# A fourth group of the u table by seven part products, its sums made on VectorE; checks moved behind other work; the last tile in its own banks

## Chip, cores and metric

One core of one Trainium2 chip runs the whole program. The metric is the device time of one execution in microseconds (us). The kernel before takes 1130.21 us, the median of three runs (1128.66 to 1132.23). TensorE is called PE here, VectorE DVE, ScalarE ACT, GpSimd POOL; SP (SyncE) issues nearly all DMAs.

## The reference

Two branches are added to the input x (2048 tokens of 512 values), both fed by its layer norm xn:

```
a, b = xn @ dft_hid_re.T, xn @ dft_hid_im.T
y    = dft_seq_re @ a - dft_seq_im @ b                 # Fourier mixing
q    = xn @ w_q                                        # 32 heads, two halves of 128
s1, s2 = q1 @ k1.T, q2 @ k2.T                          # 64 scores each, best 2 of each
top 2 of the 4 sums per head -> 64 expert numbers a token and softmax gates g
act  = gelu(xn . u[e]);  out = sum g * act * v[e]      # 4096 experts, u and v 4096 x 512
result = x + y + out
```

## The kernel before, in words

The tokens are cut into 16 blocks of 128. After a DFT part (to about 102 us) comes the **score stage** (102 to 429 us): 128 steps (eight score columns j by 16 blocks i), each 12 fp16 matmuls of 512 columns on PE, one eviction on ACT (line 952), eight MAX8 and two searches on DVE (lines 956, 960). Scores wait in 4 PSUM banks and 4 SBUF buffers, so DVE can fall some blocks behind PE. Beside it, u and v are read and split into a high and a low fp16 part: ACT writes the high parts and a scaled copy (780, 781), POOL subtracts (782).

Instead of gathering experts, the kernel then forms z = xn @ u.T for **all** 4096 experts, gates it, and multiplies with all of v. The u table has 16 groups of 256 experts. Blocks 0 and 1 are done alone (`u_part`, line 1095); then seven cycles follow, each a **pair** of blocks in z (7 x 41 us) and then two v stretches (together 45 us), `v(b-1)` and `v(b)`, and at the end `v(15)`.

Within a pair, four groups and two blocks make a 2x2 matrix product, done in Winograd's way: seven part products of 24 matmuls with 128 columns (`slot`, line 1173) instead of eight. `SEQ` writes their order by hand: `1a 5a 2a 6a c 3a ...`, where the digit is one of the seven products (`OPS`), the letter one of three such quads, and `c` a plain group (0 to 3) by `u_part`, 24 matmuls with 256 columns for both blocks at once. Between products ACT copies the running sum X out of PSUM (lines 1213, 1218, 1220, 1226: after 1, 5, 6 and 7), DVE adds (1215, 1223, 1227), ACT applies gelu (1203); product 7 must wait until the copy after 6 has read X, and 4 for the copy after 7. Products 3, 6 and 7 need sums of four u parts, which are made before, in the score stage (`sum_u`, lines 809 to 812, and `split4`, 794 and 795), kept in HBM as `s_d` and loaded by SP into a ring of three 512 KB buffers (`ring_load`, line 1156).

The gates come as `g_mm` (line 1270): DVE builds two halves, each a mask L (1260) and a weighted mask R (1265, then 1268), and PE multiplies them, 32 matmuls of 32 columns. There are three L and R buffers and two PSUM buffers for g. `w_part` then multiplies act by g (1278, DVE), rounds (1285, ACT) and takes the rest (1286, DVE). The call g(b,1) is made by `put(ph, 12, ...)` inside the pair.

Between all this stand **checks** that inputs are what the fast path assumes. A unit of U (`compare`, lines 1350 to 1405; the last four `compare_w`) reads a piece of a DFT matrix (0.5 MB), takes differences on DVE and one sum of absolute values on ACT (1404). A unit of F[0] (`fit`, 1451) reads 0.5 MB of w_q, or later of v, and takes one such sum on ACT (1456). F[1] does so for resident parts of u and v (1467). The places are listed as `put(phase, position, unit)`. Loads of both kinds and the tiles of `w_part` share four buffers (tag "w").

Every engine works its list strictly in order; a scheduler makes the lists when the program is built.

## Time and profile before

| | |
|---|---|
| median of three runs | 1130.21 us (1128.66 to 1132.23) |
| profiled execution | 1130.3 us, of which the span on the engines is 1128.0 |
| granted TensorE clock | 0.999 |
| busy share of the span | PE 98%, DVE 86%, ACT 59%, POOL 29% |
| data moved | 206.80 MB |

Times in the tables are microseconds from the start of the span. A timeline row gives start, duration, engine, line, operation, output and inputs, the number of instructions put together in the row, and in brackets the idle time before it with what ended it. PE's durations overlap each other, so a stretch of PE is measured from one start to the next.

### The profile page before, as it was taken

To read this page: it belongs to the slowest core of one execution; us is meant where nothing else is said; L and a number is where in the kernel's file an instruction comes from. 1 tells how busy PE (TensorE), PEld (TensorE's weight loads), DVE (VectorE), ACT (ScalarE), POOL (GpSimd) and SP (SyncE) were. 2 spreads that over 40 slices of the span, in tenths; PEclk is the share of its full clock that TensorE was granted. 3 is DMA by queue.
4 is the path that set the end of the run, shared out by engine and by line. 5 is a ranking of instruction groups with operands and counts; after the bars stand their busy time and mean duration, and the time that the engine had idled before them with its cause. 6 is when DMAs were issued, how large, how long until landed. Compare 5 with 4: busy or idle time off the path is not lost.

```text
span 1128.0 us, 28019 instructions
## 1 busy us (share of the span) xinstructions
PE 1109.6 (98%) x11024; PEld 720.0 (64%) x11024; DVE 965.1 (86%) x2883; ACT 667.7 (59%) x1118; POOL 328.6 (29%) x364
## 2 busy tenths in 40 slices
PE   9999999999999999999999999999999999999997
PEld 6455554544545459678479479579469569559643
DVE  7899989989889899885997996997997897887892
ACT  6557698798898465365546545535545635545442
POOL 1415998888889750000000010010010010000000
PEclk9999999999999999999999999999999999999999
DMA  9984456346353215663754854753745755655353
GB/s 285 286 209 164 162 182 202 116 156 200 97 182 111 97 52 187 214 218 118 265 205 153 255 209 141 259 203 146 272 165 189 236 192 197 225 197 188 105 186 107
DMA packets 123932, 206.80 MB, mean 183 GB/s; under 512 B 34564, under 2 KB 65419, under 8 KB 123790
## 3 DMA queue, kind: packets, MB, share of 16 engines
q1 hardware_dynamic: 123488, 204.84, 54.7%
q8 instruction: 88, 1.44, 0.5%
q14 instruction: 54, 0.44, 0.1%
q10 hardware_dynamic: 302, 0.08, 0.0%
HBM read 171.52 MB, written 27.59 MB: 177 GB/s over the span
## 4 chain that ended last, share of the span: by engine, by line
PE 46%; DVE 12%; DMA 3%; ACT 3%; POOL 2%; issue 1%; SPq 0%; ACTq 0%; DVEq 0%; POOLq 0%
PE v L1328 18%; PE z L1173 16%; PE z L1095 9%; PE g L1270 3%; DVE L L1260 2%; DVE w L1278 2%; DMA cx<-in_cb_dram 2%; DVE vals L956 1%; DVE act L1286 1%; DVE idx L960 1%; DMA fit<-in_wq_dram 1%; DVE w L1286 1%; DVE cx L1378 1%; DVE R L1265 1%; DMA v<-v_d 1%
## 5 line engine op out<-in xcount | busy, mean ns | idle before, releaser
L252 PE MATMUL s<-m,xq 128*128 128x512 f16 x1344 | 297.4, 379 | 1.0 <-ACT ss L952 0.5
L1328 PE MATMUL v<-v,act 128*128 128x512 f16 x1044 | 230.8, 379 | 0.3 <-DMA v<-v_d 0.3
L252 PEld LDWEIGHTS <-xq 128*128 128x128 f16 x1344 | 129.8, 98 | 152.2 <-issue 2.5
L1341 POOL TENSOR_TENSOR y<-y,xr 128x512 f32<-128x512 f32 x15 | 28.7, 1915 | 637.9 <-DMA y<-y_d 455.8
L1260 DVE TENSOR_TENSOR L<-io_lam,cmp 128x2048 f16<-128x2048 f16 x128 | 156.1, 1220 | 26.0 <-PE g L1270 25.9
L1328 PEld LDWEIGHTS <-act 128*128 128x128 f16 x1044 | 100.1, 98 | 116.5 <-issue 0.6
L956 DVE MAX8 vals<-ss 128x8 f32<-128x64 f32 x896 | 133.5, 216 | 3.9 <-ACT ss L952 3.9
L1095 PE MATMUL z<-xb,u 128*128 128x128 f16 (+1 forms) x1440 | 121.8, 244 | 0.1
L1173 PEld LDWEIGHTS <-u 128*128 128x128 f16 x2016 | 114.7, 98 | 3.1 <-issue 2.6
L1095 PEld LDWEIGHTS <-u 128*128 128x128 f16 x1440 | 107.6, 98 | 7.5 <-issue 0.2
L1328 PE MATMUL v<-v,w 128*128 128x512 f16 x480 | 106.3, 379 | 0.3 <-DMA v<-v_d 0.3
L952 ACT ACTIVATE ss<-s,wsc 128x512 f32<-128x512 f32 x120 | 81.4, 683 | 38.6 <-PE s L252 33.4
L1404 ACT ACTIVATE cx<-cx 128x896 f32<-128x896 f32 x64 | 60.5, 946 | 67.7 <-DVE cx L1384 38.1
L960 DVE FIND_INDEX8 idx<-vals,ss 128x8 uint16<-128x256 f32 x224 | 93.8, 419 | 0.0
L1173 PEld LDWEIGHTS <-s 128*128 128x128 f16 x1440 | 82.5, 98 | 0.2
L1328 PEld LDWEIGHTS <-w 128*128 128x128 f16 x480 | 46.0, 98 | 53.8 <-issue 0.6
L1285 ACT ACTIVATE act<-w 128x1024 f16<-128x1024 f32 x36 | 48.3, 1358 | 53.8 <-DVE w L1278 49.4
L1270 PEld LDWEIGHTS <-L 128*128 128x128 f16 x2048 | 60.5, 96 | 15.6 <-DVE R L1268 4.2
L1270 PE MATMUL g<-R,L 128*128 128x32 f16 x2048 | 62.0, 176 | 4.3 <-DVE R L1268 4.2
L1278 DVE SCALAR_TENSOR_TENSOR w<-act,scl,g 128x1024 f32<-128x1024 f32 x44 | 55.8, 1277 | 10.3 <-ACT act L1203 10.3
L1173 PE MATMUL z<-xb,u 128*128 128x128 f16 x1008 | 63.1, 219 | 0.4 <-ACT act L1102 0.3
L1173 PE MATMUL z<-x,u 128*128 128x128 f16 x1008 | 61.3, 219 | 1.6 <-ACT w L1226 0.8
(366 smaller groups left out, 1860.8 us busy)
## 6 DMA issues: line engine op xcount, KB each, us to landing
v<-v_d SPq DMA_DIRECT2D x67, 512.0 KB, 4.6
cx<-in_cb_dram SPq DMA_DIRECT2D x64, 448.0 KB, 6.1
s<-s_d SPq DMA_DIRECT2D x42, 512.0 KB, 3.1
w<-in_wq_dram SPq DMA_DIRECT2D x28, 512.0 KB, 6.3
fit<-in_wq_dram SPq DMA_DIRECT2D x28, 512.0 KB, 4.7
uv<-in_vn_dram SPq DMA_DIRECT2D x16, 512.0 KB, 3.8
uv<-in_ut_dram SPq DMA_DIRECT2D x16, 512.0 KB, 4.0
s_d<-v SPq DMA_DIRECT2D x24, 256.0 KB, 4.1
```

Of the source, the lines that this page charges most:

```text
L252: nc.tensor.matmul(ps, xt[i][:, l, kd, :], m[:, r, kd, :], start=(n == 0), stop=(n == 3 * KD - 1))
L952: nc.scalar.activation(s, ps, AF.Copy, scale=inv)
L956: nc.vector.max(vals[:, i, w, :, h], s[:, g, :])
L960: nc.vector.max_index(idx[:, i, w].rearrange("p k h -> p (k h)"), vals[:, i, w, 0:2].rearrange("p k h -> p (k h)"), s[:, w * HC:g + 1, :]. ...
L1095: nc.tensor.matmul(ps if n == 1 else ps.rearrange("p (b n) -> p b n", b=2), ug[:, l, c % 2, kd, :], xb2[:, k0, r, kd, :] if n == 1 else xb ...
L1173: nc.tensor.matmul(bank[:, t * P:(t + 1) * P], lt, rt, start=(t == k == 0 and op in "125"), stop=(t == 3 and k == 5), skip_group_check=op ...
L1260: nc.vector.tensor_tensor(L.rearrange("p t (l two) -> p t l two", two=2), io_lam.rearrange("p (l two) -> p l two", two=2).unsqueeze(1).to_ ...
L1270: nc.tensor.matmul(p[:, hf, t * NC:(t + 1) * NC], L[:, t, :], R[:, t, :], start=True, stop=True)
L1278: nc.vector.scalar_tensor_tensor(w, act[:, :, ts], fw, p.rearrange("p h (n c) -> p c (h n)", c=NC), op0=ALU.mult, op1=ALU.mult)
L1285: nc.scalar.activation(w16[..., 0], w, AF.Copy)
L1328: nc.tensor.matmul(pv, w16[:, c, :, l], v_sb[g][:, r, cc, :], start=(n + cc == 0 and k == 0), stop=(n == end and cc == 1 and k == 2))
L1404: later.append(lambda: nc.scalar.activation(tf[:, P:], tf[:, P:], AF.Abs, accum_out=chk[:, n:n + 1]))
```

## The change

Four parts. **First**, groups 0 to 3 become a fourth quad; the plain groups are gone from the pairs, `SEQ` has 28 products, and g(b,1) stands as `g` between the last 7 and the last 4. The sums of these groups are made in the score stage, by DVE in place of POOL, in the scratch of tiles of v; ACT and POOL split them like the others. **Second**, the w_q checks leave the pairs and half of those of v(0) leave too; they go to position 3 of each odd v stretch and to the start of v(2) and v(4). **Third**, the difference checks are placed anew; the last three come behind the last weights of block 15. **Fourth**, the last two 256-column halves of block 15 each get a PSUM bank of their own, after a first addition into y.

```diff
 XS = 512.0
 V1 = 5
 V2 = 9
-QUADS = (8, 10, 12, 14), (9, 11, 13, 15), (4, 5, 6, 7)
+QUADS = (0, 1, 2, 3), (8, 10, 12, 14), (9, 11, 13, 15), (4, 5, 6, 7)
 PAIRS = tuple(range(2, NT, 2))
 
 
...
             nc.gpsimd.tensor_tensor(dl, raw, dh, op=ALU.subtract)
             if which == 0 and not safe and any(g in q for q in QUADS):
                 SRAW[g] = raw
-                sum_u(g, 0)
+                if g > 3:
+                    sum_u(g, 0)
 
         def scratch(g):
             return v_sb[g].rearrange("p l c d -> p (l c d)").bitcast(F32)
...
         def sum_u(g, part, at=None):
 
             qd, t = next((n, q.index(g)) for n, q in enumerate(QUADS) if g in q)
-            par = [f for w, f in fills if w == 0 and any(f in q for q in QUADS)].index(g) % 2
-            s4 = scratch(8 - par)
+            par = [f for w, f in fills if w == 0 and f > 3].index(g) % 2 if g > 3 else g % 2
+            s4 = scratch(8 - par if g > 3 else g)
+            hi = v_sb[4 if g in (2, 3) else 6].rearrange("p l c d -> p (l c d)")
+            eng = nc.gpsimd if g > 3 else nc.vector
             if part == 0:
                 raw = SRAW.pop(g)
                 a = [raw[:, c, k * 256:k * 256 + 256] for c in range(2) for k in range(2)]
                 r = [s4[:, k * 256:k * 256 + 256] for k in range(4)]
-                nc.gpsimd.tensor_tensor(r[0], a[2], a[3], op=ALU.add)
-                nc.gpsimd.tensor_tensor(r[1], r[0], a[0], op=ALU.subtract)
-                nc.gpsimd.tensor_tensor(r[2], a[0], a[2], op=ALU.subtract)
-                nc.gpsimd.tensor_tensor(r[3], a[1], r[1], op=ALU.subtract)
+                eng.tensor_tensor(r[0], a[2], a[3], op=ALU.add)
+                eng.tensor_tensor(r[1], r[0], a[0], op=ALU.subtract)
+                eng.tensor_tensor(r[2], a[0], a[2], op=ALU.subtract)
+                eng.tensor_tensor(r[3], a[1], r[1], op=ALU.subtract)
                 return
-            split4(part - 1, s4, v_sb[6].rearrange("p l c d -> p (l c d)")[:, par * 2 * D:par * 2 * D + 2 * D],
+            split4(part - 1, s4, hi[:, par * 2 * D:par * 2 * D + 2 * D],
                    lambda i: s_d[qd].rearrange("o p (t l f) -> t l p o f", t=4, l=2)[t, i], at)
 
         def sum_x(b, part, at=None):
...
                         lambda at, j=j, t=t: m_prep(j, t, wqp, behind(sw, at)))
         fills = [divmod(n, 16) for n in (0, 1, 2, 8, 3, 10, 4, 16, 12, 14, 5, 17, 9, 11, 6, 18, 13, 15, 7, 19, 20,
                                          23, 24, 21, 22)]
-        slots = [29, 31, 36, 43, 45] + [16 * j + i for j in range(3, 7) for i in (4, 6, 11, 13)]
+        slots = [28, 31, 35, 42, 47] + [16 * j + i for j in range(3, 7) for i in (4, 6, 11, 13)]
         slots = slots[:-1] + [113] + [119 + 2 * n for n in range(4)]
         for (which, g), n in zip(fills, slots):
             todo[n].append(lambda at, w=which, g=g: fill_uv(w, g, at))
             todo[n - (3 if n < 119 else 1)].append(lambda at, w=which, g=g: fill_load(w, g))
             if which == 0 and not safe and any(g in q for q in QUADS):
+                if g < 4:
+                    todo[n + 3].append(lambda at, g=g: sum_u(g, 0))
                 todo[n + 5].append(lambda at, g=g: (sum_u(g, 1, at), sum_u(g, 2)))
         if not safe:
             for n, b in zip((19, 22, 25, 106, 109, 118, 39), PAIRS):
...
         if not safe:
             sx = stE.enter_context(tc.tile_pool(name="sx", bufs=1, side="left"))
             x4 = sx.tile([P, 2, 4, 2, P], F16, name="x4")
-            PLAIN = [g for g in range(16) if not any(g in q for q in QUADS)]
-            SEQ = "1a 5a 2a 6a c 3a 1b 7a 2b 5b 4a 6b c 3b 1c 7b 2c 5c 4b 6c c 3c 7c c 4c".split()
+            SEQ = ("1a 5a 2a 6a 3a 1b 7a 2b 5b 4a 6b 3b 1c 7b 2c 5c 4b 6c 3c 1d 7c 2d 5d 4c 6d 3d 7d "
+                   "g 4d").split()
+            NS = {"g": 800}
 
             def turn_q(k, n):
-                return ("abc" if n % 2 else "cba").index(k)
+                return ("abcd" if n % 2 else "dcba").index(k)
 
             OPS = {"1": (0, None, None, 0), "2": (1, None, None, 1), "5": (2, None, 0, None), "6": (None, 1, 1, None),
                    "3": (None, 3, None, 3), "7": (None, 2, 2, None), "4": (3, None, 3, None)}
...
             clock = 0
             for n in range(len(PAIRS)):
                 for o in SEQ:
-                    ns = 2616 if o == "c" else 1344
-                    if o != "c" and OPS[o[0]][1] is not None:
+                    ns = NS.get(o, 1344)
+                    if o not in NS and OPS[o[0]][1] is not None:
                         USES.append((clock, clock + ns, turn_q(o[1], n), OPS[o[0]][1]))
                     clock += ns
                 clock += 50000
...
 
         def z_pair(b, n, after):
 
-            cgs = iter(PLAIN)
             st = {}
             late = []
-            total, done, cg = sum(2616 if o == "c" else 1344 for o in SEQ), 0, 0
+            total, done, cg = sum(NS.get(o, 1344) for o in SEQ), 0, 0
             for at, o in enumerate(SEQ):
                 while late and late[0][0] <= at:
                     late.pop(0)[1]()
-                if o == "c":
-                    u_part(b, next(cgs))
-                    done += 2616
+                if o == "g":
+                    g_mm(b[0], 1)
+                    done += NS[o]
                 else:
                     op, qd = o[0], turn_q(o[1], n)
                     quad = QUADS[qd]
...
         def v_part(b, pv, cg):
             w16 = parts(b)
             if b + 1 == NT and cg == 7 and not safe:
+                y = Y[b]
+                nc.vector.scalar_tensor_tensor(y, pv, osc, y, op0=ALU.mult, op1=ALU.add)
                 for h in range(2):
                     d = slice(h * 256, h * 256 + 256)
+                    ph = take(f"v{b}_{h}")[0][:, 0:256]
                     for n, cc in ((14, 0), (14, 1), (15, 0), (15, 1)):
                         g = v_order(b)[n]
                         for k, (l, r) in enumerate(((0, 0), (0, 1), (1, 0))):
-                            nc.tensor.matmul(pv[:, d], w16[:, 2 * g + cc, :, l], v_sb[g][:, r, cc, d], start=False,
-                                             stop=(n + cc == 16 and k == 2), skip_group_check=True)
-                    y = Y[b]
-                    nc.vector.scalar_tensor_tensor(y[:, d], pv[:, d], osc, y[:, d], op0=ALU.mult, op1=ALU.add)
+                            nc.tensor.matmul(ph, w16[:, 2 * g + cc, :, l], v_sb[g][:, r, cc, d],
+                                             start=(n + cc == 14 and k == 0), stop=(n + cc == 16 and k == 2))
+                    nc.vector.scalar_tensor_tensor(y[:, d], ph, osc, y[:, d], op0=ALU.mult, op1=ALU.add)
                     nc.sync.dma_start(out[b * P:(b + 1) * P, d], y[:, d])
                 return
             end = 13 if b + 1 == NT and not safe else 15
...
         for ph in phases[2:]:
             if ph[0] == "z":
                 put(ph, 9, G(ph[1], 0))
-                put(ph, 12, G(ph[1], 1))
+                if safe:
+                    put(ph, 12, G(ph[1], 1))
         for b in range(13):
             put(("v", b), 3, lambda b=b: compact_d(b + 2))
         put(("z", 14, 15), 8, lambda: compact_d(15))
         if not safe:
-            for cg in (1, 3, 5, 7):
-                put(("v", 0), cg, F[0])
+            for ph, cg in ((("v", 0), 2), (("v", 0), 6), (("v", 2), 0), (("v", 4), 0)):
+                put(ph, cg, F[0])
             for ph, cg in ((("v", 12), 0), (("v", 14), 1), (("v", 14), 3), (("v", 14), 7)):
                 put(ph, cg, F[0])
             for ph in phases[3:]:
                 if ph[0] == "z":
-                    put(ph, 8, F[0])
-                    for cg in {2: (9, 11, 13, 15), 4: (9, 11, 13, 15), 14: (9, 12)}.get(ph[1], (9, 12, 15)):
+                    for cg in {2: (9, 11, 13, 15), 4: (9, 11, 13, 15), 6: (9, 11, 13, 15), 14: (9, 11)}.get(ph[1], (9, 11, 15)):
                         put(ph, cg, U)
                 elif ph[1] < 14:
                     for cg, f in enumerate((None, F[1], F[1], U, U, U, U, F[0]) if ph[1] % 2 == 0 else (
-                            None, F[1], F[0], None, U, U, U, F[0])):
-                        if f and (ph[1] < 13 or f != U or cg == 6):
+                            None, F[1], F[0], F[0], U, U, U, F[0])):
+                        if f and (ph[1] < 13 or f != U):
                             put(ph, cg, f)
             for cg in range(3):
                 put(("v", 14), cg, F[1])
-                put(("v", 14), cg + 4, U)
+                put(("v", 14 + cg // 2), (6, 7, 0)[cg], U)
                 put(("v", 15), cg, F[1])
             for f, n in ((U, 68), (F[0], NK + 16 - V2), (F[1], 16 + V2)):
                 assert sum(v.count(f) for v in plan.values()) >= n
```

The lists of three engines move as follows. The first place is DVE's list at the end of the pair (4, 5), ahead of `v(3)`: `z5_4_2` and `z5_4_3` are the products 3 of a quad, `L` and `R` the masks, `cmp4` what block 4's masks are made of, `w4_0` and `w4_1` the weighted activations. Before:

```order
L1260 TENSOR_TENSOR L1_5738<-io_lam_72,cmp4_8257 128x2048
L1265 TENSOR_TENSOR R1_5739<-io_c_73,cmp4_8257 128x512
L1260 TENSOR_TENSOR L2_5740<-io_lam_72,cmp4_8257 128x2048
L1223 TENSOR_TENSOR w4_126<-z5_4_2_8951,w4_126 128x4x128
L1268 TENSOR_TENSOR R1_5739<-R1_5739,cmp4_8257 128x512
L1265 TENSOR_TENSOR R2_5741<-io_c_73,cmp4_8257 128x512
L1268 TENSOR_TENSOR R2_5741<-R2_5741,cmp4_8257 128x512
L1227 TENSOR_TENSOR w4_126<-w4_126,act4_8399 128x4x128
L1278 SCALAR_TENSOR_TENSOR w4_0_9240<-act4_8399,scl_93,g4_0_8905 128x1024
```

And now, with lines 5 higher:

```order
L1228 TENSOR_TENSOR w4_126<-z5_4_3_9207,w4_126 128x4x128
L1265 TENSOR_TENSOR L1_5774<-io_lam_72,cmp4_8374 128x2048
L1232 TENSOR_TENSOR w4_126<-w4_126,act4_8516 128x4x128
L1270 TENSOR_TENSOR R1_5775<-io_c_73,cmp4_8374 128x512
L1265 TENSOR_TENSOR L2_5776<-io_lam_72,cmp4_8374 128x2048
L1283 SCALAR_TENSOR_TENSOR w4_0_9434<-act4_8516,scl_93,g4_0_9044 128x1024
L1273 TENSOR_TENSOR R1_5775<-R1_5775,cmp4_8374 128x512
```

The mask L1, which goes into g(4,2)'s second half, is now made after the last product 3, since its buffer is free only once PE has done the first half of the late g(4,1); and the weighted R1 has come to stand behind `w4_0`. The other six pairs have the same rows at this place.

The second place is SP's list as `v(3)` begins (`v12_3` and its like are pieces of v, `fit` a w_q check's load, `cx` the two loads of a difference check). Before:

```order
L1455 DMA fit9_9318<-in_wq_dram 128x1024
L1306 DMA v12_3_9238<-v_d_60 128x2048
L1306 DMA v13_3_9295<-v_d_60 128x2048
L1357 DMA cx15_9394<-in_ca_dram 128x128
L1358 DMA cx15_9394<-in_cb_dram 128x896
L1306 DMA v14_3_9312<-v_d_60 128x2048
L1357 DMA cx16_9414<-in_ca_dram 128x128
```

And now:

```order
L1311 DMA v12_3_9432<-v_d_60 128x2048
L1462 DMA fit7_9512<-in_wq_dram 128x1024
L1462 DMA fit8_9572<-in_wq_dram 128x1024
L1311 DMA v13_3_9489<-v_d_60 128x2048
L1311 DMA v14_3_9506<-v_d_60 128x2048
L1364 DMA cx15_9591<-in_ca_dram 128x128
L1365 DMA cx15_9591<-in_cb_dram 128x896
L1311 DMA v15_3_9526<-v_d_60 128x2048
L1364 DMA cx16_9611<-in_ca_dram 128x128
```

Two w_q loads instead of one now stand ahead of the stretch's first difference check.

The third place is DVE's list in the score stage, where the sums of group 2 are made (`v2_917` is the scratch, `uv0_2` the u rows, `ss2_4` the scores of step 4 of column 2). Before there were only the searches:

```order
L956 MAX vals2_1965<-ss2_4_2169 128x8 x5
L960 MAX_INDEX idx2_1966<-vals2_1965,ss2_4_2169 128x8
L956 MAX vals2_1965<-ss2_4_2169 128x8 x3
L960 MAX_INDEX idx2_1966<-vals2_1965,ss2_4_2169 128x8
L956 MAX vals2_1965<-ss2_5_2229 128x8 x5
```

And now:

```order
L812 TENSOR_TENSOR v2_917<-uv0_2_2017 128x256
L814 TENSOR_TENSOR v2_917<-uv0_2_2017 128x256
L959 MAX vals2_1969<-ss2_4_2186 128x8 x5
L963 MAX_INDEX idx2_1970<-vals2_1969,ss2_4_2186 128x8
L959 MAX vals2_1969<-ss2_4_2186 128x8 x3
L813 TENSOR_TENSOR v2_917<-v2_917,uv0_2_2017 128x256
L963 MAX_INDEX idx2_1970<-vals2_1969,ss2_4_2186 128x8
L959 MAX vals2_1969<-ss2_5_2247 128x8 x5
```

Four additions a group stand between the searches, 16 in all.

## The prediction

> **What bounds the kernel now.** I read the page's busy shares first, then busy time in a few stretches, then timelines.
>
> ```profile
> PE 1109.6 (98%) x11024; PEld 720.0 (64%) x11024; DVE 965.1 (86%) x2883; ACT 667.7 (59%) x1118; POOL 328.6 (29%) x364
> 102.60:429.00 326.40, 325.72 (x2207) 167.35 (x2205) 298.52 (x1565) 258.79 (x424) 264.85 (x296) 1.00 0.42 136
> 662.43:703.45 41.02, 41.02 (x703) 39.94 (x700) 31.88 (x53) 22.09 (x40) 1.27 (x1) 1.00 0.44 152
> 703.45:748.90 45.45, 45.45 (x356) 22.82 (x353) 40.39 (x63) 22.97 (x34) 1.85 (x1) 1.00 0.74 251
> ```
>
> The last three rows are the score stage, one pair and its two v stretches; after the length come the busy times of PE, weight load, DVE, ACT and POOL, then the clock, the DMA share and GB/s. PE is busy all through each of them, at full clock. So work taken from PE comes off the end, as long as DVE and ACT, which feed it, keep up: DVE has 9.1 us of idle in a pair, 5.1 us in the two v stretches, and 27.9 us in 128 score steps.
>
> **What is saved.** The PE timeline near the end of a pair:
>
> ```profile
> 606.93 2.78 PE L1095 MATMUL z<-xb,u 128*128 128x256 f16 x24
> 609.55 0.95 PE L1270 MATMUL g<-R,L 128*128 128x32 f16 x32
> 610.35 1.50 PE L1173 MATMUL z<-xb,s 128*128 128x128 f16 x24
> 611.69 1.50 PE L1173 MATMUL z<-x,s 128*128 128x128 f16 x24
> 616.99 2.75 PE L1328 MATMUL v<-v,act 128*128 128x512 f16 x12
> 619.58 0.95 PE L1270 MATMUL g<-R,L 128*128 128x32 f16 x32
> ```
>
> From start to start a plain group takes 2.62 us, a g 0.80 and a product 1.34. Four plain groups are 10.48 us, seven products 9.38: 1.10 us a pair, **7.7 us** in seven pairs.
>
> The last halves: 12 matmuls of 256 columns take half a plain group's 2.62, so the second half ought to start 1.31 us after the first, at 1120.09; it waits for DVE to read the shared bank and starts at 1120.83.
>
> ```profile
> 1118.78 1.47 PE L1316 MATMUL v<-v,act 128*128 128x256 f16 x12
> 1120.83 1.47 PE L1316 MATMUL v<-v,act 128*128 128x256 f16 x12 [0.58 <-DVE y L1319]
> 1120.29 0.48 DVE L1319 SCALAR_TENSOR_TENSOR y<-v,scl,y 128x256 f32<-128x256 f32 x1 [10.05 <-PE v L1316]
> ```
>
> Own banks save **0.74**; the added 512-wide step on DVE hides under the first half's 1.31 us. DVE idled 10.05 us before it, so the difference checks that now end later cost nothing there.
>
> Checks that stand in ACT's way go from three places:
>
> ```profile
> 471.94 1.06 ACT L1456 ACTIVATE fit<-fit 128x1024 f32<-128x1024 f32 x1 [4.93 <-DMA fit<-in_wq_dram]
> 473.00 1.32 ACT L1285 ACTIVATE act<-w 128x1024 f16<-128x1024 f32 x1
> 474.36 1.34 DVE L1286 TENSOR_TENSOR act<-w,act 128x1024 f16<-128x1024 f32 x1 [1.24 <-ACT act L1285]
> 477.53 0.56 PE L1270 MATMUL g<-R,L 128*128 128x32 f16 x16 [1.42 <-DVE R L1268]
> 850.15 1.06 ACT L1456 ACTIVATE fit<-fit 128x1024 f32<-128x1024 f32 x1 [1.97 <-DMA fit<-in_wq_dram]
> 851.84 1.33 PE L1173 MATMUL z<-x,u 128*128 128x128 f16 x21 [0.84 <-ACT w L1226]
> 1080.90 0.57 PE L1270 MATMUL g<-R,L 128*128 128x32 f16 x16 [1.14 <-DVE R L1268]
> 1089.89 0.55 PE L1270 MATMUL g<-R,L 128*128 128x32 f16 x16 [0.71 <-DVE R L1268]
> ```
>
> In v(0) a w_q check, waiting for its load, holds ACT; the rounding behind it comes late, DVE waits 1.24, PE 1.42. The check stands behind that rounding now; I take 1.3. In the pair (10, 11) the same happens to a copy: 0.84, all recovered. In v(14) DVE is late twice, 1.85 in sum; its units go behind the last weights, but DVE stays near its limit, so I take 1.1 (0 to 1.85). Together **3.2**. All savings: 7.7 + 0.74 + 3.2 = 11.6 us.
>
> **What is lost in the pairs.** The g that stood 7.4 us ahead of the pair's end stands one product (1.34) ahead now, so L1 can be built only there:
>
> ```profile
> 610.14 1.23 DVE L1260 TENSOR_TENSOR L<-io_lam,cmp 128x2048 f16<-128x2048 f16 x1 [2.02 <-PE g L1270]
> 611.28 0.42 DVE L1265 TENSOR_TENSOR R<-io_c,cmp 128x512 f16<-128x512 f16 x1
> 614.71 0.69 DVE L1227 TENSOR_TENSOR w<-w,act 128x512 f32<-128x512 f32 x1
> 617.97 2.47 DVE L1278 SCALAR_TENSOR_TENSOR w<-act,scl,g 128x1024 f32<-128x1024 f32 x2 [2.57 <-ACT act L1203]
> 614.10 0.58 ACT L1226 ACTIVATE w<-z 128x512 f32<-128x512 f32 x1
> 615.44 0.72 ACT L1203 ACTIVATE w<-w,scl 128x512 f32<-128x512 f32 x1 [0.76 <-DVE w L1227]
> 616.07 0.46 ACT L1102 ACTIVATE act<-z,scl 128x256 f32<-128x256 f32 x1
> 617.25 0.69 ACT L1203 ACTIVATE act<-z,scl 128x512 f32<-128x512 f32 x1 [0.36 <-PE z L1173]
> ```
>
> Count from v's first matmul. The g starts 2.14 before it (0.80 + 1.34); DVE starts L1 0.59 after (609.55 to 610.14), at -1.55; the add 1.14 later (to 611.28), at -0.41; its gelu 0.73 after that (614.71 to 615.44), at 0.32; the last gelu 0.63 behind (to 616.07), at 0.95, where before it began at 0.26; `w4_0` 0.72 after (617.25 to 617.97), at 1.67; done 1.24 later (half of 2.47), at 2.91. PE wants g(4,2), whose PSUM buffer `w4_0` frees and whose R1 stands behind it, at 2.59 (616.99 to 619.58). It waits some 0.34: **2.4** in seven pairs (bounds 0 and twice that). The copy after the last 7 has only the g to hide under: like the gelu at 617.25 it begins some 0.26 after the product, and takes 0.58, against 0.80: **0.3** in seven pairs.
>
> Without plain groups a copy has to be done within two products, 2.69 us, at ten places of a pair. Start, copy and gelu take 0.26 + 0.58 + 0.63, and a check's two instructions on ACT 0.95 + 0.19: 2.6. It just fits, unless the check waits for a load. In the first pair it did not fit even before:
>
> ```profile
> 501.87 0.95 ACT L1404 ACTIVATE cx<-cx 128x896 f32<-128x896 f32 x1 [1.15 <-issue]
> 502.72 0.19 ACT L1404 ACTIVATION_READ_ACCUMULATOR cx<-cx 128x1 f32 x1
> 504.54 1.50 PE L1173 MATMUL z<-x,u 128*128 128x128 f16 x24 [0.60 <-ACT act L1226]
> ```
>
> PE comes there 2.62 us sooner now (a plain group less), DVE's checks hardly do. I take **1.5** there (0 to 2.6) and **1.5** in the six other pairs (0 to 6: one late check, 0.84 as above, in each, and a little more). DVE's three added sums (3 x 0.69) and ACT's longer copies fit in their idle of 9.1 and 18.9 us a pair. The nine ring loads instead of six land in time by this row, with 6 products, 8 us, between a buffer's uses:
>
> ```profile
> s<-s_d SPq DMA_DIRECT2D x42, 512.0 KB, 3.1
> fit<-in_wq_dram SPq DMA_DIRECT2D x28, 512.0 KB, 4.7
> ```
>
> **What is lost in the v stretches.** Nine w_q checks come here (seven in odd stretches, two in v(2), v(4)). Each holds one of four shared buffers for 4.7 + 1.06 + 0.2, about 6 us, so what is queued behind on SP for a buffer, the difference checks, comes up to 6/4 = 1.5 us later. DVE takes these in order; behind them stand L and R, for which PE waits. Bounds: 0 (the 5.1 us of idle swallow it) to 9 x 1.5 = 13.5. I take **2.5**, nearer to 0, since few checks made DVE wait before.
>
> **What is lost in the score stage.** POOL gets four more subtractions of 2.13 us; DVE gets 16 sums.
>
> ```profile
> L1365 DVE TENSOR_TENSOR cx<-cx 128x256 f32<-128x256 f32 x16 | 6.5, 408 | 0.5 <-DMA cx<-in_cb_dram 0.3
> L795 POOL TENSOR_TENSOR v<-v,v 128x1024 f16<-128x1024 f32 x19 | 40.6, 2134 | 5.3 <-ACT v L794 5.3
> 213.69 2.14 POOL L782 TENSOR_TENSOR u<-uv,u 128x1024 f16<-128x1024 f32 x1
> 214.14 1.83 DVE L898 TENSOR_TENSOR z<-g,z 128x128 f16<-128x128 f32 x1
> ```
>
> Free, a sum is 0.41 us, 6.5 in all, of which 17 steps (31 to 47) with 0.22 idle each hide 3.7, and the score buffers the rest. But the last two rows show a DVE operation with two SBUF inputs, of 16k elements, that took 1.83 and ended with the POOL instruction that began before it. If each sum waits out a whole POOL instruction, it is 16 x 2.13 = 34 us; less 3.7, and less some five steps of 2.59 (13) by which DVE may fall back further before the eight score buffers are full, 17 us reach PE. Between 0 and 17 I take **0.9**, near the free end, as the sums of a group are spread over three steps. The Trainium skill's "SBUF — State Buffer", section "SBUF: two separate sides", calls this port pair of DVE and GpSimd an exclusive lock: against a GpSimd operation that reads SBUF, a DVE operation with two SBUF inputs blocks fully. These two rows agree; by that rule the dear end would be the likelier.
>
> **The sum.** Losses: 2.4 + 0.3 + 1.5 + 1.5 + 2.5 + 0.9 = 9.1; net 2.5 us less than the profiled execution of 1130.3 (span 1128.0, 2.3 around it), which is the median of the runs, 1130.21, within 0.1: **1127.8 us**.
>
> **The rivals.**
> *All is covered*: checks never late, stretches and score stage swallow theirs; only 2.4 + 0.3 is lost: -8.9, **1121.4**. For it: DVE idles in every stretch. Against: the waits at 477.53 and 851.84, one late load each.
> *The w_q checks hold the buffers* (slower): place, SP's list in the odd v stretches, ahead of the first difference check; price 13.5 in place of 2.5: **1138.8**. It decides once a difference check's load comes later than DVE's idle there can take, 5.1 us in two stretches.
> *POOL shuts DVE out*: 17 in place of 0.9: **1143.9**.
> *The change doesn't do as it says*, PE waiting for copies in each pair as long as it saves (7.7 in place of 3.0): **1132.5**.
>
> **Chances.** Forecast (1124 to 1131) 0.5; covered 0.2; w_q checks 0.15; POOL 0.06; no gain in the pairs 0.09. The range leaves out POOL and the ends of the next: 1120 to 1138. A measurement tells about 0.3%, 3.4 us, from no change: faster than 1126.8 are the covered case and under half of the forecast, 0.42; slower than 1133.6 the two dear cases and a part of the fourth, 0.23; between, 0.35.
>
> **What would show it.** A pair of 39.9 plus its waits (41.02 before), with seven waits of about 0.3 at the first g of an odd v stretch behind line 1283; the score stage still 326.4 us; no wait at the last half, in v(0) and v(14). Wrong would be: waits of over 1 us for R (1273) in odd v stretches behind a difference check, waits for copies (1225, 1231) in more than two pairs, or DVE rows of 2 us at lines 812 to 815 with ACT and PE idle after them.

## The result, and the profile after

The changed kernel takes **1164.7 us**, the median of six runs (1160.4 to 1171.0), against 1131.5 of the kernel before on the same chip: ratio 1.030, 95% interval 1.026 to 1.033. Forecast were 1127.8 us and 1120 to 1138. Its profiled execution took 1160.4 us, the fastest of the six and 30.1 more than that of before.

Page of after, first line (busy time and share of each engine), and two rows of busy time by stretch: the pair (6, 7) and its two v stretches, in the columns of the prediction's rows.

```profile
PE 1109.6 (96%) x11528; PEld 722.6 (62%) x11528; DVE 988.4 (85%) x2921; ACT 680.5 (59%) x1126; POOL 343.3 (30%) x368
671.89:717.33 45.44, 40.70 (x775) 40.11 (x771) 34.05 (x55) 22.64 (x39) 2.29 (x2) 1.00 0.55 189
717.33:765.78 48.45, 45.93 (x355) 22.84 (x353) 43.68 (x75) 24.46 (x37) 1.27 (x1) 1.00 0.67 236
```

PE is no longer busy all through. It works 40.70 of 45.44 us in the pair, and waits 2.5 in the v stretches. Divided at PE's first instruction of each stage, and at its last of all, the 30 us lie so (us, one execution each):

| stage | before | after | change | forecast |
|---|---|---|---|---|
| up to z(0) (score stage at its end) | 415.9 | 420.1 | +4.2 | +0.9 |
| z(0), z(1) | 47.6 | 47.6 | 0 | 0 |
| v(0) | 24.8 | 23.5 | -1.3 | -1.3 |
| seven pairs | 289.3 | 305.0 | +15.7 | -5.2 |
| six v stretches between them | 274.7 | 287.2 | +12.5 | +4.9 |
| v(13) to v(15) | 70.1 | 69.0 | -1.1 | -1.8 |

What PE waits for from 480 to 1100 us (waits of after: engine, line, releaser; then sum, times, longest):

```profile
PE g L1275 <- DVE R L1273: 8.9, 7, 2.4
PE z L1179 <- ACT act L1231: 7.9, 5, 2.1
PE z L1179 <- ACT w L1225: 4.3, 2, 2.2
PE z L1179 <- DMA s<-s_d: 2.5, 5, 0.9
PE v L1335 <- DMA v<-v_d: 2.4, 1, 2.4
PE z L1179 <- ACT act L1225: 2.3, 1, 2.3
```

Lines 1225 and 1231 are the copies after products 6 and 7, 1273 the weighted mask. How a copy comes late shows the timeline of after in the pair (6, 7):

```profile
689.98 1.03 DVE L1385 TENSOR_TENSOR cx<-cx 128x512 f32<-128x512 f32 x2 [0.94 <-DMA cx<-in_cb_dram]
691.60 0.28 DVE L1391 TENSOR_TENSOR cx<-cx 128x128 f32<-128x128 f32 x1
691.91 0.95 ACT L1411 ACTIVATE cx<-cx 128x896 f32<-128x896 f32 x1 [3.27 <-DMA cx<-in_cb_dram]
692.86 0.58 ACT L1225 ACTIVATE act<-z 128x512 f32<-128x512 f32 x1
693.49 1.50 PE L1179 MATMUL z<-x,s 128*128 128x128 f16 x24 [2.28 <-ACT act L1225]
697.97 0.95 ACT L1411 ACTIVATE cx<-cx 128x896 f32<-128x896 f32 x1 [0.29 <-DVE cx L1410]
698.91 0.58 ACT L1231 ACTIVATE act<-z 128x512 f32<-128x512 f32 x1
699.54 1.50 PE L1179 MATMUL z<-x,u 128*128 128x128 f16 x24 [1.88 <-ACT act L1231]
```

ACT stands 3.27 us at the sum of a difference check: its load came late, so DVE ended the differences only at 691.88. The copy that PE needs is queued behind that sum. The loads, in SP's list:

```profile
672.92 0.33 SPq L1347 DMA_DIRECT2D xr<-in_x_dram  x1
673.87 0.34 SPq L1353 DMA_DIRECT2D out_dram<-y  x1
678.19 0.33 SPq L1345 DMA_DIRECT2D y<-y_d  x1
...
682.41 0.34 SPq L1347 DMA_DIRECT2D xr<-in_x_dram  x1
682.85 0.86 SPq L1162 DMA_DIRECT2D s<-s_d  x2
...
684.23 0.42 SPq L1365 DMA_DIRECT2D cx<-in_cb_dram  x1
```

The chain of the v part before (store the block, load y into the same tile, load the input rows into theirs) holds SP until 682.41, 10.5 us into the pair; ring loads and checks follow in a burst. But this is as old as the kernel. Timeline of before at the same place, with the first such load at 673.59, 11.2 us into its pair (12.3 in after):

```profile
673.59 0.42 SPq L1358 DMA_DIRECT2D cx<-in_cb_dram  x1
...
680.59 2.78 PE L1095 MATMUL z<-xb,u 128*128 128x256 f16 x24
...
681.10 0.95 ACT L1404 ACTIVATE cx<-cx 128x896 f32<-128x896 f32 x1 [1.01 <-issue]
682.62 0.59 ACT L1220 ACTIVATE act<-z 128x512 f32<-128x512 f32 x1
683.21 1.50 PE L1173 MATMUL z<-xb,s 128*128 128x128 f16 x24
```

The sum and the copy behind it ran late there too; a plain group stood on PE meanwhile, and the next product began the moment the copy ended, without a wait.

In the v stretches it is DVE that waits for a difference check's load; from there to the mask R at 764.85 it is busy almost without a gap, and PE waits for the mask. Timeline of after (line 1463 is the sum of a w_q check):

```profile
744.00 0.47 SPq L1365 DMA_DIRECT2D cx<-in_cb_dram  x1
746.17 1.03 DVE L1385 TENSOR_TENSOR cx<-cx 128x512 f32<-128x512 f32 x2 [2.62 <-DMA cx<-in_cb_dram]
761.56 1.04 ACT L1463 ACTIVATE fit<-fit 128x1024 f32<-128x1024 f32 x1
764.85 0.47 DVE L1273 TENSOR_TENSOR R<-R,cmp 128x512 f16<-128x512 f16 x1
765.38 0.55 PE L1275 MATMUL g<-R,L 128*128 128x32 f16 x16 [2.37 <-DVE R L1273]
```

In the score stage the longest wait, 1.87 us, is for POOL's piece of the routing matrix. Timeline of after:

```profile
162.16 2.13 POOL L782 TENSOR_TENSOR u<-uv,u 128x1024 f16<-128x1024 f32 x1
162.22 2.14 DVE L922 SCALAR_TENSOR_TENSOR di<-c,i2s 128x64 int32<-128x64 f32 x1 [0.21 <-POOL i2s L918]
168.86 0.32 POOL L899 TENSOR_TENSOR g<-c,g 128x64 f32<-128x64 f32 x1 [0.78 <-DVE g L898]
169.13 2.13 POOL L167 TENSOR_TENSOR w<-w,wh 128x1024 f16<-128x1024 f32 x1
171.32 0.20 PE L148 MATMUL m<-sums,w 128*128 128x64 f16 x1 [1.87 <-POOL w L167]
```

A tiny DVE operation (64 elements a partition) took 2.14 us beside POOL's subtraction; in before the same operation, with no such subtraction beside it, took 0.23. The gates' chain, which goes from DVE to POOL, came later by that and by the added sums; POOL waited in it for 0.78 and split the matrix late.

### The profile page after: what moved, and what is told of

It is laid out like the page before. It is cut to its first block, busy times and chain, and to the rows that moved or that the text cites. A ratio compares the mean times of both kernels' runs of the same rounds, so it can differ in the third digit from the quotient of the medians.

```text
span 1158.2 us, 29173 instructions
## 1 busy us (share of the span) xinstructions
PE 1109.6 (96%) x11528; PEld 722.6 (62%) x11528; DVE 988.4 (85%) x2921; ACT 680.5 (59%) x1126; POOL 343.3 (30%) x368
## 4 chain that ended last, share of the span: by engine, by line
PE 28%; DVE 23%; DMA 10%; ACT 4%; POOL 3%; issue 2%; SPq 1%; ACTq 0%; DVEq 0%; POOLq 0%
PE z L1179 14%; PE v L1335 9%; DVE L L1265 5%; DMA cx<-in_cb_dram 3%; DMA cx<-in_ca_dram 3%; DVE w L1283 3%; PE z L1100 3%; PE g L1275 2%; DVE cx L1385 2%; DVE vals L959 2%; DVE act L1291 2%; DVE idx L963 2%; DVE R L1270 1%; ACT cx L1411 1%; DVE R L1273 1%
## 5 line engine op out<-in xcount | busy, mean ns | idle before, releaser
L1348 POOL TENSOR_TENSOR y<-y,xr 128x512 f32<-128x512 f32 x15 | 31.9, 2127 | 663.0 <-DMA y<-y_d 276.0
L1179 PEld LDWEIGHTS <-u 128*128 128x128 f16 x2688 | 154.6, 98 | 12.6 <-issue 12.0
L1179 PEld LDWEIGHTS <-s 128*128 128x128 f16 x1944 | 110.5, 98 | 11.1 <-issue 7.3
L1179 PE MATMUL z<-x,u 128*128 128x128 f16 x1344 | 82.5, 220 | 10.9 <-ACT act L1231 7.9
L1179 PE MATMUL z<-x,s 128*128 128x128 f16 x1296 | 81.2, 219 | 7.8 <-ACT w L1225 4.3
L1179 PE MATMUL z<-xb,u 128*128 128x128 f16 x1344 | 85.2, 221 | 0.0
L1208 ACT ACTIVATE act<-act,scl 128x512 f32<-128x512 f32 x56 | 40.1, 721 | 60.5 <-DVE act L1228 32.7
L1291 DVE TENSOR_TENSOR act<-w,act 128x1024 f16<-128x1024 f32 x44 | 58.3, 1326 | 5.3 <-ACT act L1290 5.3
```

The source lines that it names most:

```text
L1179: nc.tensor.matmul(bank[:, t * P:(t + 1) * P], lt, rt, start=(t == k == 0 and op in "125"), stop=(t == 3 and k == 5), skip_group_check=op ...
L1208: nc.scalar.activation(d, d if src is None else src, AF.Gelu_apprx_tanh, scale=zsc)
L1291: nc.vector.tensor_tensor(w16[..., 1], w, w16[..., 0], op=ALU.subtract)
```

## The experiments

Times are medians, ratios against the kernel before run beside them; stage lengths come from one profiled execution each, and since executions of a kernel that waits much differ by up to 1% (after: 1160.4 to 1171.0), a few us in a sum are not read. "V" is the sum of the six v stretches, "pairs" that of the seven pairs (before: 289.3 and 274.7; after: 305.0 and 287.2).

One cause of this spread shows in the traces. In 13 of the 20 profiled executions PE's granted clock falls to 0.5 for spells of 3.41 us (some of 6.83 or 10.24) from the score stage to the last v stretches, 34 in all; in the 3.41 us ahead of each, PE had stood idle for 1.6 to 3.3. After has one such spell, from 948.4, where two products start 2.35 us apart in place of 1.34. A spell that PE works through costs about 1.7 us, half its length (an estimate). Not every wait of 2 us is followed by one: after has eleven waits of 1.4 to 2.4 us with none behind them, and its one spell follows two of 0.36 and 1.24. So part of a sum can be this, and where it changes a reading it is given below. Before, and the runs of after with one kind of check left out, have none; after's 305.0 would be 303.2 without its one.

### Without the checks

```diff
         def compare(n):
+            return
...
         def compare_w(n):
+            return
...
         def fit(n):
 
+            if 0 < n < NK:
+                later.append(lambda: nc.vector.tensor_copy(fits[:, n:n + 1], fits[:, 0:1]))
+                return
```

The kernel after without difference checks and with one of 28 w_q checks:

> The changed kernel without any difference check and with 27 of 28 w_q checks left out. Theories A and C: pairs 40.4 us, stretches 45.5, so 305 + 287 becomes 283 + 274: about 1130 us. Theory B: pairs and stretches each keep half or more of what they lost, total above 1147.

1127.2 us, 0.9963 (0.9949 to 0.9977). A pair takes 40.03 (the first 39.23), a v stretch 45.74. The same left out of the kernel before:

> The kernel before without its difference checks and with 27 of its 28 w_q checks left out (their results copied from the first); all else as before. It is the control for the same cut in the kernel after, which gave 40.03 us a pair and 45.74 a v stretch at 1127.2 us. Theory 1, four plain groups cover the checks, and only seven products without checks show what the fourth quad itself is worth: all seven pairs at 41.02, all odd-even v stretches at 45.45, v(0) near 23.5, the total some 2 to 3 us below before (1128 to 1129), so that the quad itself saves 0.99 less 0.29 a cycle, 4.9 us in seven. Rival, the checks slow the kernel before as well, by loads and engine time spread over all stages: pairs below 41.02, the total below 1124, and then the quad itself would be worth less or nothing.

1126.9 us, 0.9966 (0.9951 to 0.9982): pairs 41.02, V 272.7. So in itself the fourth quad gives 0.99 a pair and takes 0.29 a v stretch, as forecast (1.10 less 0.11 for the last copy; 0.34). Without the checks the two kernels take the same time, so the 33 us go with the checks. The score stage's loss stays (PE waits 1.9 for the matrix and 2.2 for score buffers in the first); it takes, with the v stretches, most of what the pairs save. (Left out of this: z(0) and z(1) take 6.7 and 4.2 us more in the two runs; in the first the verdict's reductions, released early, hold DVE there, an effect of the missing checks.)

Only the 24 difference checks of the pairs left out, then only 27 w_q checks:

> The changed kernel without the 24 difference checks that stand in the pairs (left out altogether). Theory C, ACT's copies wait behind the sums of difference checks whose loads are late: the pairs fall from 305 us in sum to 7 x 40.4 = 283, total about 1142 us, and no wait of PE for a copy above 0.3 us is left. Theory B: pairs stay above 42 us, with PE waiting for s (the ring) or copies late without a check ahead of them.

> The changed kernel without the loads and sums of 27 of the 28 w_q checks (their results are copied from the first). Theory A: v stretches 45.5 us each, 12 us less in sum; the pairs, in which no w_q check stands, stay near 305 us in sum; total about 1152. Theory B: stretches stay near 48 us, total above 1160.

Without the first, 1138.4 us (1.0063, 1.0034 to 1.0092), pairs 283.7, V 285.0; without the second 1147.0 (1.0149, 1.0113 to 1.0185), pairs 298.2, V 279.3. The pairs lose 21.2 by their difference checks.

### Is it the places, or the lost cover?

The quad with the checks at the places of before, and the places (with the own banks) without the quad:

> The changed kernel with the checks put where they stood before (one w_q check in each pair, four in v(0), difference checks at 9, 12, 15). Theory A, the moved w_q checks fill the four shared buffers and SP's list in the v stretches: the seven stretches of two v blocks go from 47 to 48.4 us each back to 45.5, about 12 us less in sum, v(0) is 1.3 longer; the pairs stay at 42 to 45 us; total some 1152 us. Theory B, everything is late because a pair has nine ring loads instead of six: the stretches stay at 48 and the total at 1163 to 1168.

> The kernel before, three quads and four plain groups in each pair, g(b,1) early, with the second, third and fourth part of the change alone (all checks at the places of after, the last halves in own banks). Theory 5: the checks' loads come as late here as in after, but a plain group behind a product gives a copy 2.6 us more, so PE does not feel it: pairs 287 to 290 (41.0 to 41.4 each), while the v stretches lose to the moved w_q loads what they lost in after without the late mask: 282 to 286 in place of 274.7; total 1134 to 1141. Rival: the new places make the pairs slow, cover or not: pairs 295 to 303, total above 1144.

The first takes 1155.0 us (1.0217, 1.0180 to 1.0253), pairs 300.0, V 281.8, so the old places give back 5 us in each, where theory A had 12 in the v stretches and none in the pairs; the second 1146.6 (1.0123, 1.0098 to 1.0147), V 296.8. Busy time by stretch of the second, a pair and its v stretches:

```profile
852.54:893.56 41.02, 41.02 (x703) 39.94 (x700) 31.71 (x52) 20.98 (x38) 1.35 (x1) 1.00 0.42 140
893.56:942.95 49.39, 47.17 (x356) 23.26 (x353) 41.16 (x68) 23.93 (x36) 1.27 (x1) 0.97 0.70 241
```

With plain groups a pair hides the same checks whole: 41.02 here, and all seven are 290.6, of which 3.4 are two spells of the halved clock behind waits in the v stretches; seven times 41.02 is 287.1. Without plain groups a pair doesn't hide them, at the old places or the new. The v stretches lose by the plan alone, 22 us in this execution (3.2 of it by two spells; the clock of 0.97 in the second row is one), more than forecast (7 to 11). Each part loses by itself.

### Loads or engine time?

In the pairs, the difference checks read resident memory in place of their two loads (the verdict then sees other data, so the program's second path runs behind; only the first path is read, and the total, 1819.5 us, says nothing; `rs` is true in the pairs, and `rf` is what the differences then read):

```diff
+            if rs:
+                rf = u_sb[0].rearrange("p l c k e -> p (l c k e)").bitcast(F32)
...
+            else:
+                nc.sync.dma_start(tf[:, :P], ca[ri, g, :, kk * P:(kk + 1) * P])
+                nc.sync.dma_start(tf[:, P:], cb[ri, g, kk].rearrange("p b c -> p (b c)"))
```

> The kernel after, where the 24 difference checks of the pairs read resident memory (the u table as f32) in place of their two loads; their DVE and ACT instructions, their places and their buffers stay. Theory 1, a pair loses because a check's loads come late and its sum on ACT, waiting, stands ahead of a copy that PE needs: the pairs come near those without checks, 40.0 to 41.0 each, their sum 281 to 286 in place of 305, the total 1138 to 1145. Theory 2, the two products between a product and the reuse of its bank are too short for a check's own work on ACT (0.95 and 0.19) and DVE, loads or not: the pairs stay at 42 to 45.5, their sum above 298, the total above 1155. In between, 286 to 298, both have a part, in the proportion of the sum. The v stretches stay at 285 to 288 in either case, as the w_q checks there are untouched.

```profile
667.60:708.67 41.07, 40.56 (x774) 40.07 (x771) 32.63 (x49) 22.45 (x39) 2.31 (x2) 1.00 0.50 158
```

Pairs 288.4: of the 21.2 the loads make 16.5, the checks' own work on ACT and DVE 4.7. Both theories have a part, the loads four fifths. The same for the w_q checks (one sum of resident memory in place of a load):

> The kernel after, where 27 of the 28 w_q checks read resident memory in place of their load; their sum on ACT, their buffer (held now for about 1.1 us in place of 6) and their places stay; the number that goes into the verdict is copied from the first. It tells apart what the w_q checks cost: left out whole they gave back 7.9 us in the v stretches (287.2 to 279.3) and 6.8 in the pairs. Theory 4, as predicted: the load holds one of four shared buffers and SP behind it, so the difference checks come later; then v stretches 279 to 282, pairs 296 to 300, total 1146 to 1150. Rival: it is ACT's time (1.06 each, in front of gelus and roundings): v stretches 285 to 288, pairs above 302, total above 1157.

```profile
718.37:764.10 45.73, 45.60 (x355) 22.81 (x353) 44.17 (x76) 23.53 (x35) 1.56 (x1) 1.00 0.63 204
```

V 278.9: the loads make 8.3 of the 12.5, the sums on ACT nothing to be seen (the run without the checks had 279.3). The pairs stayed at 305.3 and the time at 1156.9 (1.0193, 1.0139 to 1.0247; single executions 1143.9 to 1160.3), as the rival had it. But these pairs hold three spells of the halved clock, 5.1 us, where after has one and the run without w_q checks none: without the spells they are 300.1, 303.2 and 298.2. So 5.1 of the 7.1 us by which this run and the one without the checks differ in the pairs are the clock.

### Why are the loads late?

Three runs move them. Store, y and input rows by POOL's queue in place of SP's:

```diff
-            nc.sync.dma_start(y, y_d[b])
+            (nc.sync if safe or b + 1 == NT else nc.gpsimd).dma_start(y, y_d[b])
...
-            nc.sync.dma_start(xr, x[b % 4, b // 4])
+            (nc.sync if safe or b + 1 == NT else nc.gpsimd).dma_start(xr, x[b % 4, b // 4])
...
-            nc.sync.dma_start(out[b * P:(b + 1) * P], y)
+            (nc.sync if safe or b + 1 == NT else nc.gpsimd).dma_start(out[b * P:(b + 1) * P], y)
```

> The kernel after, where the store of a finished block, the load of y and the load of the input rows (the chain store, y, input, each waiting for the one ahead of it) are issued by POOL's queue in place of SP's; POOL is idle there. Theory 1a, SP's list is held by this chain at the start of every pair and in each v stretch, so that the loads of the checks behind it come late: SP's long waits (8.1 us at 672.92) vanish, the checks' loads of a pair are issued from 1 to 5 us after its start in place of 12 to 17, the pairs' sum falls from 305 to 285 to 293, the v stretches from 287 to 278 to 283, the total to 1137 to 1150. Rival 1b, the loads come late because they wait for one of the four shared buffers, or for the DMA engines, whoever is ahead of them on SP: pairs above 300, v stretches above 285, the total within 5 us of after.

1153.1 us (1.0201, 1.0156 to 1.0247): pairs 296.0, V 288.8. The first check's load goes out 7.7 to 9.6 us into a pair, not 12 to 17 as I had put it for after (it was 9.9 to 12.3). The chain on SP makes 9 us of the pairs (11 without the spells) and nothing in the v stretches. PE's waits for ring loads in the pairs, 2.5 us in after, are gone. The checks' loads themselves by POOL:

> The kernel after, where the loads of all w_q, v and difference checks (except the four of the window) are issued by POOL's queue in place of SP's; POOL is idle in these stages but for two additions. Everything is still checked. Theory 1c: the loads come late because SP issues them in one list with ring loads, v loads and the chain of store, y and input, each waiting for something; on a list of their own they wait only for their buffer: pairs 283 to 292 (as without loads, 288), v stretches 278 to 284, total 1135 to 1147. Rival 1b: their own buffers, each held by a late sum on ACT, make them late: pairs 296 to 305, v stretches 285 to 289, total 1150 to 1165. A load by POOL costs about 0.55 us of POOL; if it also takes longer to land, pairs above 305.

1178.8 us (1.0408, 1.0378 to 1.0439): pairs 301.9 (of which 8.7 are spells of the halved clock, behind PE's longer waits), V 309.3. This theory fell in the v stretches. POOL's waits show why (from 480 to 1100 us):

```profile
POOL fit L1462 <- ACT fit L1474: 123.8, 6, 29.7
POOL y L1348 <- DMA y<-y_d: 109.2, 9, 14.9
POOL fit L1462 <- ACT cx L1411: 67.6, 13, 13.5
```

POOL's list is in order as well: a load that waits for one of the four shared buffers, or an addition that waits for y, holds every load behind it. Next, each difference check issuing the load of the next one:

> The kernel after, where each difference check issues the loads of the next one, a position ahead of its own work; nothing is left out. A buffer is so held longer, and the loads stand further ahead in SP's list. Theory 1a: the place in SP's list makes the loads late; then the checks of a pair start with their data there, pairs 286 to 296 in place of 305, v stretches 283 to 288, total 1143 to 1156. Rival 1b: one of four shared buffers held longer makes other loads and the tiles of w_part wait: v stretches 290 to 305, pairs 300 to 306, total above 1165.

1153.6 us (1.0182, 1.0158 to 1.0206): V 281.1, pairs 304.3. In the v stretches the place in SP's list counts for 6 us; in the pairs nothing is won; the chain still stands in SP's list there, which I take for the reason without a run that shows it. The Trainium skill's "DMA: Bandwidth & Descriptors", section "Issuing engines are not separate DMA queues", says that issuing from several engines only saves the little time of issuing. No run here tests bandwidth; the gain of 9 us and the loss of 22 came from what each list waits for (an issue of the chain took SP 0.33 to 0.42 us, while the chain held its list for 10.5).

### The late mask

```diff
-            SEQ = ("1a 5a 2a 6a 3a 1b 7a 2b 5b 4a 6b 3b 1c 7b 2c 5c 4b 6c 3c 1d 7c 2d 5d 4c 6d 3d 7d "
-                   "g 4d").split()
+            SEQ = ("1a 5a 2a 6a 3a 1b 7a 2b 5b 4a 6b 3b 1c 7b 2c 5c 4b 6c 3c 1d 7c 2d 5d g 6d 3d 7d "
+                   "4c 4d").split()
```

> The kernel after with another end of the written order: the late g(b,1) stands behind product 5 of the last quad (4.8 us before the pair's end in place of 2.1), and product 4 of the quad before it comes in its place between the last 7 and the last 4. The theory of the late mask: L1 of the next g waits for the first half of this g, so the first g of the odd v stretch waits 0.29 to 0.30 us in all seven cycles and the last 4 another 0.11; with the g earlier both go: each is 0, v stretches 2.0 us less in sum (285), pairs 0.8 less, total 1161 to 1163. Rival: the gelus of product 4, now later, or DVE's list, from which the masks take time ahead of the additions, cost as much as is saved: total 1164 to 1168. The pairs' long waits of 1 to 2.5 us for copies are not touched by it in either case.

1158.5 us (1.0240, 1.0214 to 1.0267), better than forecast. The waits of 0.29 at the first g are gone in all seven cycles; the 0.11 at the last 4 became 0.15; pairs 300.2. V, at 288.2, holds 1.9 us of the halved clock; the 286.3 that are left are 0.9 less than after's, where 2.0 were forecast.

### The score stage

The 16 sums by POOL:

> The kernel after, where the 16 sums of groups 0 to 3 in the score stage are made by POOL in place of DVE; the rest as after. Theory 3, the 4 us that the score stage lost come from DVE: a sum that begins beside a POOL instruction takes up to 2 us, the gates' chain goes from DVE to POOL and back, and POOL, waiting in it, splits the routing matrix late, for which PE waits 2.03 us at 169.26; then the sums on POOL (0.76 us each, 12 in all, spread over 60 us) free DVE, that wait goes and the first z begins at 416 to 418 in place of 420.1, the total 2 to 4 us below after. Rival, the four added splits (2.13 us each) make POOL late whoever makes the sums: the wait at 169 stays or grows, z begins at 420 to 426, the total the same as after or longer.

1169.8 us (1.0335, 1.0290 to 1.0380): z(0) begins at 425.5. PE's wait for the matrix grew:

```profile
172.78 0.20 PE L148 MATMUL m<-sums,w 128*128 128x64 f16 x1 [4.54 <-POOL w L167]
```

So the sums on DVE are the better of the two; POOL, with four subtractions more, is what comes late. How much of the 4.2 the subtractions alone make was not tried. This run's pairs are the same program as after's, yet its execution has 314.6 us in them: 9.7 are five stretches of halved clock, and 304.9 are left against 303.2. Two more spells, 3.2 us, lie behind the waits for the matrix.

### Can the quad pay with everything kept?

After with g early, the chain by POOL's queue, and the nine moved w_q checks in z(0) and z(1):

> The kernel after with what helped it, and nothing left out: g early and product 4 late at a pair's end, store and y and input by POOL's queue, and the nine moved w_q checks in the first two blocks (seven in z(0), two in z(1)), where ACT has 10 us of idle in 24 and the DMA engines are at 0.23. If the effects add: v stretches 287 - 8 - 2 = 277 to 282, pairs 305 - 9 - 4 = 286 to 294, the score stage as in after, total 1132 to 1144: still not faster than before, as the pair's own saving of 7 us is smaller than score stage (4), late loads in the pairs and v stretches together. Rival, the loads of difference checks simply shift, and what one move gains the next wait takes: total above 1148.

1151.4 us (1.0174, 1.0151 to 1.0197): pairs 288.7 and V 276.5 as hoped, but z(0) and z(1) take 62.9 in place of 47.6. Four w_q checks in z(0) do the same to the kernel before (with the own banks and the last checks moved):

> The kernel before with the last halves in own banks, the last three difference checks behind the last weights, and the four w_q checks of v(0) in z(0), positions 0 to 3, where ACT and the DMA engines have room and the shared buffers are free. Theory: the checks cost nothing there (z(0) and z(1) stay at 47.6 us), v(0) at 23.5, pairs 287.5 to 289.5, v stretches 274 to 275, the tail 1 to 1.5 less; total 1126 to 1128, the ratio 0.9950 to 0.9975, faster than both kernels. Rival: a sum of 1.06 on ACT ahead of a gelu of z(0) holds a bank of PE: z(0) and z(1) 48.5 to 51, total 1129 to 1132.

1139.7 us (1.0070, 1.0052 to 1.0088); z(0) and z(1) take 58.6. Its timeline:

```profile
438.82 1.97 SPq L1306 DMA_DIRECT2D v<-v_d  x3
440.83 2.23 SPq L1457 DMA_DIRECT2D fit<-in_wq_dram  x4
447.66 1.06 ACT L1458 ACTIVATE fit<-fit 128x1024 f32<-128x1024 f32 x1 [10.95 <-DMA fit<-in_wq_dram]
450.55 2.47 DVE L1278 SCALAR_TENSOR_TENSOR w<-act,scl,g 128x1024 f32<-128x1024 f32 x2 [10.23 <-DMA fit<-in_wq_dram]
451.89 0.59 PE L1270 MATMUL g<-R,L 128*128 128x32 f16 x16 [4.38 <-DVE w L1278]
```

Idle engines and free buffers did not help: the loads were written for the first half of z(0) (from 416) and went out at 440.83, behind SP's loads of v, which had waited till 438.82. ACT waited 10.95 us and PE behind it. It is the mechanism of the pairs once more. Behind the waits the granted clock is 0.50 from 450.30 to 460.54; PE works 3.6 us of these, so about 1.8 of the 11 us lost are the clock. So the same with the w_q checks in the pairs:

> As the run before it of the quad with its helps (g early, product 4 late, store, y and input by POOL's queue, the difference checks at the places of after), with the nine w_q checks in the pairs, one at position 8 of each and one more in (4, 5) and (14, 15), in place of z(0) and z(1), where their loads stood behind SP's list and cost 15.4. Nothing is left out. If what that run showed of pairs (288.7) and v stretches (276.5) holds and a w_q check in a pair without plain groups costs 0.5 to 1.2: pairs 293 to 299, v stretches 276 to 278, z(0) and z(1) at 47.6, the score stage 4 more than before, total 1138 to 1145, so slower than before by 0.6 to 1.1%. If the quad could pay with everything checked, the total would be below 1128: pairs at 284 or less, which needs the w_q sums to find room between the copies.

**1134.6 us** (1.0025, 1.0010 to 1.0040), better than expected. Busy time by stretch, pair (6, 7) and its v stretches:

```profile
665.63:706.85 41.22, 40.40 (x775) 40.04 (x772) 35.37 (x59) 23.48 (x41) 2.91 (x4) 1.00 0.64 215
706.85:752.32 45.47, 45.47 (x356) 22.80 (x354) 41.12 (x70) 23.66 (x36) 2.91 (x4) 1.00 0.71 240
```

V is at 274.2, as before, pairs at 289.4 (in the fastest of its ten executions, 1131.7). No spell of the halved clock is left. Thirty of the 33 us are back, and every check is made. What remains is the score stage (3.8); in the pairs the saving of 7 goes into waits still. One thing stays open: from (4, 5) on the first difference check's load of a pair goes out 10.7 to 11.2 us in, as in before and in the midst of after's 9.9 to 12.3. So the hour of that load alone doesn't set the loss; where ACT's sums then fall between the copies must count too, and no run moved these apart.

### The pieces that helped, on the kernel before

Own banks for the last halves, the last difference checks behind the last weights, v(0) with two w_q checks, the other two in the pairs (4, 5) and (6, 7); then (14, 15) in place of (6, 7):

> The kernel before, plain groups and all, with only three small pieces of the change: the last halves in own banks, two checks of v(0) left at positions 2 and 6 and the other two put into the pairs (4, 5) and (6, 7), and the last three difference checks behind the last weights. Theory: where a pair has plain groups, they cover a check, so the two moved ones cost nothing there, and the three waits that the prediction named go: 0.7 at the last half, 1.3 in v(0), 1.0 to 1.6 in v(14); the pairs stay at 289 to 290, the v stretches at 273 to 275, total 1127.0 to 1128.5, the ratio 0.996 to 0.998. Rival: a check in a pair costs there what it cost in v(0), 0.8 to 1.3 each: pairs 291 to 292, total 1129 to 1131.

> The kernel before with the last halves in own banks, the last three difference checks behind the last weights, and of the four w_q checks of v(0) two at positions 2 and 6, one in the pair (4, 5), where it cost nothing, and one in the pair (14, 15), which has only two difference checks, in place of (6, 7), where it cost 1.3. Theory: pairs 288 to 289, v stretches 273 to 275, v(0) at 23.5, the tail 68.5; total 1126.5 to 1128.5, the ratio 0.9955 to 0.9975. Rival: the late loads of the pair (6, 7) and the following ones come from other checks shifting along, wherever the two stand: pairs 289.5 to 291, total 1129 to 1131.

1129.9 us (0.9981, 0.9969 to 0.9993), in the rival's range, and **1128.6 us** (0.9975, 0.9958 to 0.9993), at the upper end of the forecast. Both beat both kernels, the one before by 0.2%, which the intervals barely part from no change; in the first the pair (6, 7) took 42.35, so a second w_q check isn't free in every pair.

## Why the prediction was wrong

**Right.** The saving in a pair (40.03 without checks); the late mask (0.34 forecast, though its count, 2.91 less 2.59, gives 0.32; 0.29 measured); v(0) (1.3); the last halves, now one row without a wait:

```profile
717.33 2.75 PE L1335 MATMUL v<-v,w 128*128 128x512 f16 x12
720.21 0.95 PE L1275 MATMUL g<-R,L 128*128 128x32 f16 x32
1113.10 0.55 PE L1275 MATMUL g<-R,L 128*128 128x32 f16 x16 [1.34 <-DVE R L1273]
1149.47 2.78 PE L1324 MATMUL v<-v,act 128*128 128x256 f16 x24
```

From v's start to the first g it is 2.88, where it was 2.59. Of v(14)'s 1.1 little came: one wait of 1.34 stayed. The copy after the last 7 cost 0.11 a pair, not 0.04.

**Wrong: the pairs.** The step that failed is "**1.5** in the six other pairs (0 to 6: one late check, 0.84 as above, in each, and a little more)". Against the pair without checks, the six lost 23.2 and the first 2.4. The condition was named, "unless the check waits for a load", and then priced by the two waits that PE showed before. But PE's rows could not show how often the loads were late, since plain groups covered it. DVE's rows could. Waits of before, 480 to 1100 us:

```profile
DVE cx L1378 <- DMA cx<-in_cb_dram: 13.7, 19, 2.2
DVE sums L1359 <- DMA cx<-in_ca_dram: 7.0, 9, 1.1
```

Twenty-eight waits, 20.7 us, were on the trace, against "few checks made DVE wait before". Half of them lie in the pairs (14, 8.4 us), half in the v stretches. So these rows named the mechanism, but not its size: with the cover gone the difference checks cost the seven pairs 21.2, of which the loads make 16.5, and that only the runs showed. The ring loads, which were to "land in time", came late too, by 2.5 us in the pairs.

**Wrong in size: the v stretches.** 2.5 was taken for the w_q checks, with 13.5 as the dear end; the rival at 1138.8 was the true case for this stage: 12.5 in all, 8.3 of it by their loads, some 2 by the late mask. Whether these loads did it by the buffers they hold, as the rival said, or by their place in SP's list was not parted; that loads issued a check earlier gave back 6 us points to the list.

**Wrong in place: the score stage.** 0.9 was taken for sums on DVE that reach PE by the score buffers; it lost 4.2, of which 1.9 came over POOL and the routing matrix, a path that I had not followed; PE's waits by the score buffers went from 0.5 to 2.0. What the dear end feared, a DVE operation that lasts as long as POOL's beside it, was there in two of the 16 sums (2.18 and 1.94 us) and in the gates' chain (the 2.14 beside 2.13 above).

**Wrong in the form.** The three dear cases stood as alternatives, each with its chance. Here they came together: 20.9 in the pairs, 7.6 in the v stretches, 3.3 in the score stage and 0.7 in the rest, more than the terms gave, are the 32.5 from -2.5 to +30.

## What to carry to other kernels

When filler work is taken off the engine that bounds, read how late the others already were behind it: their own waits for loads, not the bound engine's, show what the filler hides. They don't give its price; here that took runs without the checks and without their loads. A load's place in an in-order issue list, behind stores and refills that wait, can decide when it lands; free buffers and idle engines at the spot where it is written did not help here. And losses in different stages add up; they are not rivals.

## What was not expected of the hardware

A DVE operation of 64 elements a partition took 2.14 us beside a POOL subtraction of 2.13 that began 0.06 before it, and 0.23 in the kernel before without one. A store and two loads a block by POOL's queue in place of SP's were worth 9 us in seven pairs, while POOL needed 0.55 us to issue each; with a list that waits for buffers the same queue lost 22 in the v stretches. And a PE wait can cost more than its length: behind 34 stretches with 1.6 to 3.3 us of idle in 3.41, the granted clock was 0.5 for 3.41 us or more, some 1.7 us each where PE worked.
